# Full 128-row transposes and 64x64 feed-forward tiles in an RWKV-7 and hardswish kernel

## The chip, the cores and the metric

The kernel runs on one core of one Trainium2 chip. The metric is the device time of one execution in microseconds, taken as the median of several runs; less is better. One profiled execution stands beside the runs, and all rows below come from it.

## The reference

There are two parts. The first is a recurrence over 768 time steps, for 4 batches of 8 heads of width 40. The second is a feed-forward layer over its 3072 output rows. All of it is float32.

```python
for t in range(S):                       # state: (B, H, D, D), D = 40
    y[:, :, t] = einsum('bhd,bhde->bhe', rt, state)
    Sa = einsum('bhde,bhe->bhd', state, at)
    state = state * wt[:, :, None, :] - einsum('bhd,bhe->bhde', Sa, bt) \
          + einsum('bhd,bhe->bhde', vt, kt)
# x = y as (B*S, H*D) = (3072, 320)
h = x @ w_in                             # 320 x 2048
out = (h * clip(h + 3, 0, 6) / 6) @ w_out   # 2048 x 320
```

## The kernel before

**Units.** The 768 steps are cut into 12 blocks of 64. A unit is one block of 64 steps for two batches (128 rows: two batches of 64 steps) and all 8 heads; there are 24 units, in six groups of four (NU = 4). Inside a unit the recurrence is solved as matrix products: decay products along the block (stages W, gam), turned copies of the inputs (stages A, B, K, RT, VT, S, factor), scores between them (F, E, C, H), the inverse of a triangular matrix for the whole group (invert, on VectorE, and third_block, on TensorE), the solved vectors (U, UT), the output (rS, y) and the new state (in y).

**Turning.** TensorE turns an input from rows of time to rows of features with a transpose against an identity. turn_pairs (L524) does it with four 128x128 transposes into one bank. turn_halves (L534) does it with eight 64-row transposes, one per batch, into a pair of banks. turn_in chooses by a flag. The same choice stands, written out, in factor_stage (L703 halves, L708 full) and in s_S (L943 halves, L946 full). Units 4 and later take halves in RT and VT, units 8 and later in B, factor and S (A in units 8 to 11), units 12 and later in K. From unit 8 the inputs R, and from unit 12 the inputs A, are turned by VectorE instead (L475, L478).

**Feed-forward.** feed_forward is a generator of TensorE pieces. A unit has two jobs. A job expands (L1147, tile h): for each of two column halves c, eight 128x128 products on the features 0 to 255 (two row groups), and then the last 64 features (function short): eight products of 64 rows, from win2, with c = 0 on partitions 0 to 63 and c = 1 on 64 to 127. Then ScalarE (L1162) and VectorE (L1163) make gt, and contract (L1188, tile o) multiplies by w_out, eight products of 320 columns. Tile h has room for one job, so the next job's L1147 waits for this job's L1163. The list narrow holds the waiting short of a job; it may be called ahead of its turn.

**The steady part.** From unit 4 each unit is four blocks; block m runs parts of the unit being solved (own) and of a unit being prepared (ahead). Blocks are written out by together: it goes through a list of stage names (TURNS first, then one of two NARROW lists), calls each stage up to its TensorE work, and keeps count of PSUM banks. Five are there for it: a bank one, and two pairs of two banks. A stage in TURNS takes the bank one, then halves of a pair; a stage in NARROW takes part of a pair. When five would be exceeded, finish is called: all stages begun so far issue their copies out of PSUM, in the order of the list RESULTS, and the count starts again. At the end of a block finish is called as well. Between the blocks, feed issues as many feed-forward pieces as the digit of GAPS says, and after each piece as many VectorE steps of the inversion (L803, L809) as the digit of INVERSION says. Every engine executes its own instructions in the order in which they were issued.

**Queues.** Stage move issues four copies of the finished output into the feed-forward's input xt from ScalarE's queue (L1091), and move2 four more from SP's; stage beside issues one from SP's (L1031); fetch issues the input loads, on SP's queue in the steady part.

The choice of where short goes, in together, and the count of banks for a turn:

```python
            if name == NARROW[order][0] and narrow and spread[0] and stages:
                narrow[0]()
            for stage in stages.get(name, []):
                if name in TURNS:
                    need = 2 * (open_half[0] is None) if ring[0][0] == "pair" else 1
```

Of the kernel before, what the change touches and what calls it, by code (L numbers as in the profile page):

```python
# [16 lines left out]
P = 128  # L17
# [3 lines left out]
SLOT = 64  # L21
# [10 lines left out]
def kernel(  # L32
# [42 lines left out]
    nc = tc.nc  # L75
    B, H, T, D = r.shape
# [501 lines left out]

    def prepare(i, F):
        n, o = i % NU, data[i]  # L580
        halves = i >= 2 * NU
        def w_stage():
            wt = turn_pairs(o["WN"])
            yield PE
# [145 lines left out]
                fetch(name, following(i))  # L730

        def k_stage():
            by_halves = i >= 3 * NU
            x = turn_in(o["KN"], by_halves)
            yield PE
            kt = o["kt"] = turned("kt")
            for y, z, g in zip(parts_of(kt, by_halves), x, parts_of(o["rg"], by_halves)):
                nc.vector.tensor_tensor(out=y, in0=z, in1=g, op=ALU.mult)
# [143 lines left out]
    def step(i):  # L882
# [8 lines left out]
        def s_RT():  # L891
            m["RT"] = turned("RT")
            if blocked("R", i):
                turn_blocks(m["RT"], o["RN"], "R")
            else:
                x = turn_in(o["RN"], halves)
                yield PE
                for y, z in zip(parts_of(m["RT"], halves), x):
                    nc.scalar.activation(out=y, in_=z, func=AF.Copy)
            if i:  # L900
                fetch("R", i + 1)
            if fresh:
                nc.gpsimd.tensor_copy(last_dec[p][:], dec[:, 1])
                return
            scale = tmp.tile([P, 2, NPR], F32, name="scale", bufs=2)
            nc.gpsimd.tensor_tensor(out=scale[:], in0=last_dec[p][:], in1=dec[:, 0], op=ALU.mult)
            nc.gpsimd.tensor_copy(last_dec[p][:], dec[:, 1])
            nc.vector.tensor_tensor(out=st[:, :, :, 0:D], in0=st[:, :, :, 0:D],
                                    in1=_ap(scale[:], 0, [[NPR, 2], [1, NPR], [0, D]]), op=ALU.mult)
# [15 lines left out]
            nc.vector.tensor_tensor(out=R, in0=rp[2], in1=o["EV"][:], op=ALU.add)  # L925

        def s_VT():
            x = turn_in(VN, halves)
            yield PE
            m["VT"] = turned("VT")  # L930
            for y, z in zip(parts_of(m["VT"], halves), x):
                nc.scalar.activation(out=y, in_=z, func=AF.Copy)  # L932

        def s_S():

            halves = i >= 2 * NU
            sp = ps_pair(4, SLOT) if halves else ps_any([P, 2, 2, P])
            for q in range(2):
                for j in range(2):
                    x = st[:, q, 2 * j:2 * j + 2, :].rearrange("p r d -> p (r d)")  # L940
                    if halves:
                        for s in range(2):
                            nc.tensor.transpose(out=sp[s][:, 2 * q + j, :], in_=x[half(s)],  # L943
                                                identity=ident[half(s), half(s)])
                    else:
                        nc.tensor.transpose(out=sp[:, q, j, :], in_=x, identity=ident[:])  # L946
            yield PE
            S = m["S"] = grp.tile([P, 2, 2, P], F32, name="S", tag="S", bufs=1)
            if halves:
                nc.scalar.activation(out=S[:].rearrange("p q j (s e) -> p s (q j) e", s=2), in_=sp[2], func=AF.Copy)  # L950
            else:
                nc.scalar.activation(out=S[:], in_=sp[:], func=AF.Copy)
# [188 lines left out]
    def expand(xt, j0, gts):  # L1141

        hp = [pools["h"].tile([P, NQ, P], F32, name="h", tag="h", bufs=2) for _ in range(2)]
        begun = [0, 0]

        def add(c, i, lhsT, rhs):
            nc.tensor.matmul(out=hp[c][:, i, :], lhsT=lhsT, rhs=rhs, start=(begun[c] == 0),  # L1147
                             stop=(begun[c] == 3 * NQ - 1))
            begun[c] += 1

        def short():
            narrow.clear()
            for i in range(NQ):
                for c in range(2):
                    add(c, i, win2[half(c), (j0 + i) * P:(j0 + i + 1) * P], xt[half(c), 2, :])
            if begun[0] + begun[1] == 6 * NQ:
                results()

        def results():
            for c in range(2):  # L1160
                gt = ffn.tile([P, NQ, P], F32, name="gt", bufs=4)
                nc.scalar.activation(out=gt[:], in_=hp[c][:], func=AF.Relu, bias=three[:], scale=1.0)  # L1162
                nc.vector.scalar_tensor_tensor(out=gt[:], in0=gt[:], scalar=6.0, in1=hp[c][:],  # L1163
                                               op0=ALU.min, op1=ALU.mult)
                gts.append(gt)

        narrow.append(short)
        for c in range(2):
            for t in range(2):
                for i in range(NQ):  # L1170
                    j = c * HJ + j0 + i
                    add(c, i, win[:, t, j * P:(j + 1) * P], xt[:, t, :])
                if c == 1 and t == 1 and not narrow:
                    results()
                yield True
        if not spread[0] and narrow:
            short()
            yield True
# [219 lines left out]
    for _ in range(18):  # L1398
# [7 lines left out]
    OWN_STAGES = [["RT", "VT"], ["R", "C", "S", "beside"], ["U", "UT", "rS"], ["H"], ["y"], ["move", "move2"]]  # L1406
    AHEAD_STAGES = [["W", "gam"], ["A", "B"], ["F"], ["K", "factor"], ["E"], [], [], ["EV"]]
    CLOSE_STAGES = [["W", "gam"], ["A", "B"], ["F", "K", "factor"], ["E"], [], ["EV"]]
    TURNS = ["W", "S1", "K1"]
    NARROW = [["RT1", "VT", "A1", "B", "factor", "y", "EV", "R", "C", "U", "UT", "rS", "H", "E", "F", "K", "S"],  # L1410
             ["B", "A1", "S", "VT", "E", "U", "K", "C", "y", "factor", "H", "R", "UT", "RT1", "rS", "EV", "F"]]
    RESULTS = ["C", "S", "RT1", "RT", "VT", "y", "S1", "R", "W", "A1", "move", "A", "EV", "B", "move2", "U",
              "UT", "rS", "K", "H", "K1", "factor", "E", "gam", "F", "beside"]
    FIRST_OTHER = {"RT": 2 * NU, "A": 3 * NU, "K": 3 * NU, "S": 2 * NU}
    WIDTH = {"R": NPR * D, "U": NPR * D, "y": NPR * BOTH, "EV": NPR * D}
    BLOCKS = 4
# [1 line left out]
    def together(stages, order):  # L1418
# [14 lines left out]
        for name in products:  # L1433
            if name == NARROW[order][0] and narrow and spread[0] and stages:
                narrow[0]()
            for stage in stages.get(name, []):
                if name in TURNS:
                    need = 2 * (open_half[0] is None) if ring[0][0] == "pair" else 1
                else:
                    width = WIDTH.get(name, NPR * BL)  # L1440
                    need = 2 * (shared[0] is None or shared[1] + width > 512)
                if banks + need > 5:
                    finish()
                    banks, need = 0, 1 if name in TURNS else 2
                banks += need
                rest = stage()
                next(rest)
                begun.append((name, rest))
# [36 lines left out]
    for t in (by_v, by_u):  # L1485
        nc.gpsimd.memset(t[:, :, 0:BL], 0.0)
    del score[1:]
    GAPS = "71052314311277562421243135343899422124213525759654324442543253966531154234264363"
    INVERSION = "00000000000034230000000000221223000000000012232300000000001323230000000000122343"
    m = 0  # L1490
    for i in range(NU, NK):
        spread[0] = i >= 2 * NU - 1
# [54 lines left out]
```

## Time and profile before

| what | value |
|---|---|
| runs, median (lowest to highest) | 791.65 us (790.71 to 793.52) |
| span of the profiled execution | 791.4 us |
| TensorE busy | 719.5 us, 91% of the span |
| VectorE busy | 507.2 us, 64% |
| ScalarE busy | 298.1 us, 38% |
| feed-forward, 128-row expand (L1147) | 1536 instructions, mean 282 ns |
| feed-forward, 64-row expand (L1147) | 768 instructions, mean 294 ns |
| feed-forward, contract (L1188) | 768 instructions, mean 443 ns |
| halved turns L534, L703, L943 | 448, 128 and 128 transposes |

The page gives no time of the profiled execution apart from its span; the span lies 0.2 us under the median of the runs. A float32 product shows as two TensorE instructions, a transpose as one. The mean time of a TensorE instruction is longer than the step from one to the next, since they overlap: what a group costs is read from the start of the group to the start of the next. The share of busy time is not the same all along: over the stretch from 332.7 to 791.4 us TensorE is busy for 451.8 of 458.7 us, over the one from 195.5 to 332.7 us for 125.0 of 137.2 us.

### The profile page before, as it was taken

How to read it: one execution, taken by the hardware profiler on the slowest of the kernel's cores; microseconds unless marked ns; L12 is line 12 of the kernel's file. 1: busy time of each engine (PE TensorE's matmuls, PEld its weight loads, DVE VectorE, ACT ScalarE, POOL GpSimd, SP SyncE). 2: the span in 40 equal slices, each digit the busy share in tenths (PEclk: the TensorE clock that was granted, in tenths of full speed). 3: DMA queues.
4: the chain of work that ended last, by engine and by line, in shares of the span. 5: the costliest groups of instructions: out<-in, count | busy, mean ns of one | idle time of the engine just before them, and what ended most of it. 6: DMA issues, size and time to landing. Idle time of an engine off the chain costs nothing.

```text
span 791.4 us, 32710 instructions
## 1 busy us (share of the span) xinstructions
PE 719.5 (91%) x14440; PEld 608.4 (77%) x14440; DVE 507.2 (64%) x1018; ACT 298.1 (38%) x632; POOL 166.5 (21%) x312
## 2 busy tenths in 40 slices
PE   4725778999899898999999999999999999999998
PEld 3625676878778786888888888888888888888886
DVE  7898877689455598655698556997436892233110
ACT  2347653221544422542423553234453323422111
POOL 6403012421222321222202222213212201000000
PEclk9856879999999899999999999999999999999999
DMA  9683653420334421444331344323332201211000
GB/s 122 126 193 86 155 141 59 79 45 9 53 70 72 77 53 32 84 78 85 65 64 34 76 79 94 66 47 64 67 69 58 47 14 42 46 38 28 20 9 17
DMA packets 196414, 52.74 MB, mean 67 GB/s; under 512 B 179632, under 2 KB 194992, under 8 KB 196272
## 3 DMA queue, kind: packets, MB, share of 16 engines
q1 hardware_dynamic: 188648, 47.28, 31.0%
q10 hardware_dynamic: 7624, 3.36, 1.6%
q8 instruction: 114, 1.87, 1.0%
q14 instruction: 28, 0.23, 0.1%
HBM read 38.67 MB, written 3.93 MB: 54 GB/s over the span
## 4 chain that ended last, share of the span: by engine, by line
PE 71%; DVE 15%; issue 4%; DMA 3%; ACT 2%; SPq 2%; POOL 0%; ACTq 0%; DVEq 0%; POOLq 0%
PE h L1147 25%; PE o L1188 24%; PE pair L562 4%; PE pair L1043 3%; DVE prod L803 3%; DVE x L809 3%; PE pair L534 2%; SPq L508 2%; DMA raw<-in_moe_w_out_dram 2%; PE pair L961 2%; PE one L524 1%; DVE prods L599 1%; PE pair L997 1%; PE pair L981 1%; PE pair L921 1%
## 5 line engine op out<-in xcount | busy, mean ns | idle before, releaser
L1147 PE MATMUL h<-xt,win 128*128 128x128 f32 (+1 forms) x2304 | 252.1, 286 | 5.8 <-DVE gt L1163 5.8
L1147 PEld LDWEIGHTS h<-xt,win 128*128 128x128 f32 (+1 forms) x2304 | 233.7, 195 | 22.7 <-DVE gt L1163 7.0
L1188 PE MATMUL o<-wout,gt 128*128 128x320 f32 x768 | 229.7, 443 | 0.8 <-ACT ys L1003 0.8
L1188 PEld LDWEIGHTS o<-wout,gt 128*128 128x128 f32 x768 | 139.3, 191 | 52.3 <-issue 1.1
L1163 DVE SCALAR_TENSOR_TENSOR gt<-gt,h 128x512 f32<-128x512 f32 x96 | 61.6, 682 | 107.2 <-ACT gt L1162 107.2
L1162 ACT ACTIVATE gt<-h,three 128x512 f32<-128x512 f32 x96 | 61.4, 684 | 135.1 <-PE h L1147 115.1
L803 DVE TENSOR_TENSOR prod<-x 128x30 f32<-128x30 f32 (+9 forms) x180 | 66.8, 371 | 6.5 <-POOL x L788 1.3
L809 DVE TENSOR_TENSOR x<-x,prod 128x30 f32<-128x30 f32 (+9 forms) x180 | 65.0, 361 | 5.9
L575 DVE COPY_PREDICATED store<-mask,pair 128x512 f32<-128x512 int32 x40 | 29.2, 730 | 54.8 <-PE pair L562 41.5
L1051 POOL TENSOR_TENSOR yg<-ys,gam 128x512 f32<-128x512 f32 x20 | 25.4, 1272 | 149.7 <-DVE ys L1050 87.2
L723 POOL TENSOR_TENSOR KBt<-K,rgt 128x320 f32<-128x320 f32 x19 | 16.7, 880 | 149.9 <-ACT rgt L712 146.3
L599 DVE TENSOR_TENSOR_SCAN prods<-wm,start 128x528 f32<-128x528 f32 x24 | 34.1, 1428 | 12.4 <-ACT wm L596 12.0
L1043 PE MATMUL pair<-store,KBt 64*64 64x104 f32 x1280 | 32.6, 251 | 0.6 <-ACT F L693 0.6
L610 DVE TENSOR_TENSOR_SCAN wm<-wm,start 128x528 f32<-128x528 f32 x24 | 30.6, 1277 | 0.8
L1043 PEld LDWEIGHTS pair<-store,KBt 64*64 64x64 f32 x1280 | 29.2, 133 | 1.5 <-ACT F L693 0.7
L757 ACT ACTIVATE EV<-pair 64x320 f32<-64x320 f32 x44 | 18.9, 430 | 28.8 <-PE pair L752 25.2
L642 POOL TENSOR_TENSOR at<-at,gam 128x512 f32<-128x512 f32 x12 | 15.2, 1269 | 65.5 <-DVE at L478 61.5
L950 ACT ACTIVATE S<-pair 128x512 f32<-128x512 f32 x16 | 9.6, 597 | 48.1 <-DVE store L575 27.2
L932 ACT ACTIVATE VT<-pair 128x512 f32<-128x512 f32 x22 | 13.1, 598 | 33.4 <-PE pair L562 18.0
L871 ACT ACTIVATE tinv<-pair 32x256 f32<-32x256 f32 x48 | 17.9, 374 | 19.3 <-PE pair L861 15.3
L1206 ACT ACTIVATE ob<-o 128x320 f32<-128x320 f32 x22 | 9.6, 437 | 40.7 <-issue 25.9
L783 DVE STREAM_TRANSPOSE fb<-F 128x1024 f32<-128x1024 f32 x6 | 13.0, 2159 | 17.8 <-ACT F L693 15.7
(289 smaller groups left out, 1044.7 us busy)
## 6 DMA issues: line engine op xcount, KB each, us to landing
R<-in_r_dram SPq DMA_DIRECT2D x156, 40.0 KB
A<-in_a_dram SPq DMA_DIRECT2D x61, 80.0 KB
V<-in_v_dram SPq DMA_DIRECT2D x96, 40.0 KB
out_dram<-ob SPq DMA_DIRECT2D x47, 80.0 KB
B<-in_b_dram SPq DMA_DIRECT2D x42, 80.0 KB
store<-V SPq DMA_DIRECT2D x20, 160.0 KB
W<-in_w_dram SPq DMA_DIRECT2D x37, 80.0 KB
K<-in_k_dram SPq DMA_DIRECT2D x37, 80.0 KB
```

Source lines behind the costliest of these rows:

```text
L562: nc.tensor.matmul(out=o[i][half(q), n, :], lhsT=lhs[half(i, D), n ^ (2 * q * swap), half(q)], rhs=rhs[half(i, D), n ^ (2 * q * back), hal ...
L575: nc.vector.copy_predicated(out=x[:, :, 0:BL].rearrange("p (h i) t -> p i h t", i=2), mask=mask8, data=o[2])
L599: nc.vector.tensor_tensor_scan(out=prods[:].rearrange("p r m i -> p (r m i)"), data0=wm[:, 0:SCAN], data1=start[:], initial=0.0, op0=ALU.m ...
L610: nc.vector.tensor_tensor_scan(out=back, data0=back, data1=start[:], initial=0.0, op0=ALU.mult, op1=ALU.add)
L803: nc.vector.tensor_tensor(out=pv, in0=_ap(x[:], (i + 1) * L + i, [[L, n], [0, i]]), in1=_ap(x[:], i * L, [[0, n], [1, i]]), op=ALU.mult,)
L809: nc.vector.tensor_tensor(out=rest, in0=rest, in1=pv, op=ALU.add)
L1043: nc.tensor.matmul(out=y[q][half(s), pr, :], lhsT=o[name][half(q), h * D:h * D + SLOT], rhs=m[name][half(q), x, :], start=(name == "K" and ...
L1051: nc.gpsimd.tensor_tensor(out=yg[:], in0=m["ys"][:].rearrange("p r q t -> p r (q t)"), in1=o["G"][:], op=ALU.mult)
L1147: nc.tensor.matmul(out=hp[c][:, i, :], lhsT=lhsT, rhs=rhs, start=(begun[c] == 0), stop=(begun[c] == 3 * NQ - 1))
L1162: nc.scalar.activation(out=gt[:], in_=hp[c][:], func=AF.Relu, bias=three[:], scale=1.0)
L1163: nc.vector.scalar_tensor_tensor(out=gt[:], in0=gt[:], scalar=6.0, in1=hp[c][:], op0=ALU.min, op1=ALU.mult)
L1188: nc.tensor.matmul(out=op[:], lhsT=gts[c][:, n, :], rhs=wout[:, c * HJ + r * NQ + n, :], start=((split or r == 0) and c == 0 and n == 0), ...
```

## The change

- The flags of the halved turns are set to False, so all turns from unit 4 on that TensorE makes are four 128x128 transposes (L524, L708, L946).
- short issues sixteen products of 64 rows by 64 columns instead of eight of 64 rows by 128 columns: each of the former is cut in two column halves z. The 128 moving columns stay.
- TURNS now holds ten names, so in a block the turns come first, then short, then the products; both NARROW lists and RESULTS have a new order.
- A turn that would take the bank one while the count is not zero forces finish (1 + 5 * (banks > 0)).
- GAPS and INVERSION have other digits.

```diff
     def prepare(i, F):
         n, o = i % NU, data[i]
-        halves = i >= 2 * NU
+        halves = False
...
         def k_stage():
-            by_halves = i >= 3 * NU
+            by_halves = False
...
-                x = turn_in(o["RN"], halves)
+                x = turn_in(o["RN"], False)
...
         def s_VT():
-            x = turn_in(VN, halves)
+            x = turn_in(VN, False)
...
         def s_S():
-            halves = i >= 2 * NU
+            halves = False
...
         def short():
             narrow.clear()
             for i in range(NQ):
+                for z in range(2):
+                    for c in range(2):
+                        j = (j0 + i) * P
+                        nc.tensor.matmul(out=hp[c][half(z), i, :], lhsT=win2[half(c), j + z * SLOT:j + (z + 1) * SLOT],
+                                         rhs=xt[half(c), 2, :], start=(begun[c] == 0),
+                                         stop=(begun[c] == 3 * NQ - 1))
                 for c in range(2):
-                    add(c, i, win2[half(c), (j0 + i) * P:(j0 + i + 1) * P], xt[half(c), 2, :])
+                    begun[c] += 1
...
-    TURNS = ["W", "S1", "K1"]
-    NARROW = [["RT1", "VT", "A1", "B", "factor", "y", "EV", "R", "C", "U", "UT", "rS", "H", "E", "F", "K", "S"],
-             ["B", "A1", "S", "VT", "E", "U", "K", "C", "y", "factor", "H", "R", "UT", "RT1", "rS", "EV", "F"]]
-    RESULTS = ["C", "S", "RT1", "RT", "VT", "y", "S1", "R", "W", "A1", "move", "A", "EV", "B", "move2", "U",
-              "UT", "rS", "K", "H", "K1", "factor", "E", "gam", "F", "beside"]
+    TURNS = ['RT1', 'A1', 'W', 'B', 'S', 'K1', 'VT', 'factor', 'S1', 'K']
+    NARROW = [['UT', 'E', 'C', 'U', 'H', 'EV', 'R', 'F', 'y', 'rS'], ['y', 'C', 'U', 'E', 'UT', 'H', 'EV', 'R', 'rS', 'F']]
+    RESULTS = ['C', 'RT', 'beside', 'S1', 'R', 'E', 'A1', 'RT1', 'factor', 'A', 'K1', 'B', 'move', 'UT', 'EV', 'W', 'U', 'move2', 'rS', 'K', 'S', 'y', 'gam', 'H', 'VT', 'F']
...
-                    need = 2 * (open_half[0] is None) if ring[0][0] == "pair" else 1
+                    need = 2 * (open_half[0] is None) if ring[0][0] == "pair" else 1 + 5 * (banks > 0)
...
-    GAPS = "71052314311277562421243135343899422124213525759654324442543253966531154234264363"
-    INVERSION = "00000000000034230000000000221223000000000012232300000000001323230000000000122343"
+    GAPS = '80052314141177681321243134362899422124213425759654314542433363975621173033562253'
+    INVERSION = '00000000000033230000000000221223000000000012232310010000002312330000010000131334'
```

More of the change, by code (lines that the diff above doesn't have):

```diff
@@ L895, in s_RT @@
             else:
-                x = turn_in(o["RN"], halves)
+                x = turn_in(o["RN"], False)
                 yield PE
-                for y, z in zip(parts_of(m["RT"], halves), x):
+                for y, z in zip(parts_of(m["RT"], False), x):
                     nc.scalar.activation(out=y, in_=z, func=AF.Copy)
@@ L927, in s_VT @@
         def s_VT():
-            x = turn_in(VN, halves)
+            x = turn_in(VN, False)
             yield PE
             m["VT"] = turned("VT")
-            for y, z in zip(parts_of(m["VT"], halves), x):
+            for y, z in zip(parts_of(m["VT"], False), x):
                 nc.scalar.activation(out=y, in_=z, func=AF.Copy)
         def s_S():
-            halves = i >= 2 * NU
+            halves = False
             sp = ps_pair(4, SLOT) if halves else ps_any([P, 2, 2, P])
```

## The prediction

> **What bounds the kernel.** I read the busy shares first, then the busy time of each engine by stretch, then TensorE's timeline.
>
> ```profile
> PE 719.5 (91%) x14440; PEld 608.4 (77%) x14440; DVE 507.2 (64%) x1018; ACT 298.1 (38%) x632; POOL 166.5 (21%) x312
> ...
> PE 71%; DVE 15%; issue 4%; DMA 3%; ACT 2%; SPq 2%; POOL 0%; ACTq 0%; DVEq 0%; POOLq 0%
> ```
>
> The second line is the chain that ended last. By stretch (busy time of PE, PEld, DVE, ACT, POOL, then the granted clock):
>
> ```profile
> 195.50:217.60 22.10, 19.10 (x503) 16.05 (x501) 11.09 (x19) 12.81 (x28) 7.12 (x12) 1.00 0.27 47
> 217.60:247.00 29.40, 28.01 (x654) 22.40 (x652) 15.69 (x30) 12.53 (x31) 8.11 (x14) 1.00 0.43 77
> 247.00:272.50 25.50, 23.19 (x546) 19.48 (x544) 12.65 (x23) 12.38 (x31) 7.27 (x14) 0.87 0.38 69
> 272.50:332.70 60.20, 54.68 (x1077) 46.21 (x1077) 50.28 (x107) 20.64 (x44) 14.51 (x26) 0.97 0.30 57
> 332.70:791.40 458.70, 451.80 (x8632) 381.24 (x8628) 255.11 (x508) 160.61 (x349) 79.92 (x139) 1.00 0.27 53
> ```
>
> From 332.7 us on TensorE is the bound: a microsecond more of its work is one more of time. I call this stage E. The four before it, A to D, hold units 4 to 8; TensorE waits in them, and twice its clock is granted at half. Before 195.5 us only the form of short differs, beside VectorE's chain (the L803 and L809 steps fill VectorE until 193.5 us); I cost that at nothing, and at 14 x 0.1 = 1.4 us of gain if TensorE were the bound there.
>
> Timeline, TensorE alone:
>
> ```profile
> 508.39 1.16 PE L1147 MATMUL h<-xt,win 64*128 64x128 f32 x16
> 509.39 0.41 PE L534 MATMUL pair<-ident,B 64*128 64x64 f32 x8
> 509.63 0.41 PE L943 MATMUL pair<-ident,state 64*128 64x64 f32 x8
> 509.98 0.69 PE L562 MATMUL pair<-RT,VT 40*64 40x64 f32 x32
> ...
> 218.77 0.60 PE L524 MATMUL one<-ident,W 128*128 128x128 f32 x4
> 219.21 3.40 PE L1188 MATMUL o<-wout,gt 128*128 128x320 f32 x12
> ...
> 499.85 1.61 PE L1043 MATMUL pair<-store,KBt 64*64 64x104 f32 x64
> 501.39 1.34 PE L1188 MATMUL o<-wout,gt 128*128 128x320 f32 x4
> ```
>
> From start to start: short takes 1.00 us, a halved turn 0.24 (followed by the same shape) or 0.35 (followed by 64x64 tiles), so a change of shape costs about 0.10. A full turn followed by full-size work takes 0.44. y takes 1.54.
>
> **The parts of the change.**
>
> Turns: 448 + 128 + 128 halved transposes, 8 to a turn, are 88 turns. Each costs 0.44 instead of 0.24: +0.20, together +17.6 us of TensorE; 62 of them lie in E, +12.4. The copies out of PSUM keep their sizes.
>
> Changes of shape: a halved turn stood between full-size work and 64x64 products, a third shape. In the built programs the changes between neighbours fall from 343 to 275, of these 47 in E: -4.7 us. [...]
>
> Short: 32 instructions instead of 16. No row has 64x64 tiles of 128 columns. The nearest is y: 64 instructions of 104 columns in 1.44 us without the change after it, 22.5 ns each. Scaled by 128/104 that is 27.7 ns, 0.89 us a short, -0.11. From below, 22.5 ns as it stands: 0.72, -0.28. From above, as if the halves did not run abreast, today's 62.5 ns each: 2.00, +1.00. With 34 shorts in E: -3.7 us, bounds -9.5 and +34. I take -3.7, since y uses the same four tiles in the same rotation.
>
> So E has 12.4 - 4.7 - 3.7 = +4.0 us of work. Its waits before (groups whose start-to-start time is over the sum of their instructions) add up to 4.8 us, the largest 1.1 at 394 us and 0.9 at 341.8. In the new order the turns for C are copied earlier, which ends the first kind (1.6 us). New ones come from RESULTS: S is now copied after move. Units with a third_block in their second block make L861 reuse the pair of S. I put E's waits at 2.5, that is -2.3. E: +1.7.
>
> Stage A, first block of unit 4. R is now turned ahead of W, both into the bank one, and the new count forces finish between them. In the built program W's transpose waits for ScalarE's copy of R. That copy stands behind other work:
>
> ```profile
> 195.71 2.12 ACT L824 ACTIVATE tinv<-tb 32x1024 f32<-32x1024 f32 x2 [7.99 <-DVE tb L812]
> 197.87 1.26 ACT L1162 ACTIVATE gt<-h,three 128x512 f32<-128x512 f32 x2
> 199.02 0.60 ACT L899 ACTIVATE RT<-pair 128x512 f32<-128x512 f32 x1
> ```
>
> R's turn ends at 196.1, its copy at 199.62: TensorE idles 3.5 us, with V and eight feed-forward products behind W. W's copy and scan start only 0.3 us later than before, so the chain on VectorE is hardly late, and the moved work fills waits that were there (1.4 at 206.9, 0.5 at 212, 1.4 at 213; of which 0.85 and 0.7 remain). Following each instruction to the next short I get 2.1 us late at 218.6 instead of 216.5, the five turns of A included. The other end for this wait is nothing, were the copy of R issued ahead. Then the clock:
>
> ```profile
> 302.50:306.00 3.50, 0.47 (x4) 0.47 (x5) 3.31 (x9) 0.00 (x0) 0.00 (x0) 1.00 0.24 37
> 306.00:309.40 3.40, 3.40 (x31) 3.18 (x29) 2.90 (x11) 0.00 (x0) 0.00 (x0) 0.50 0.00 0
> ...
> 305.53 3.71 PE L1147 MATMUL h<-xt,win 128*128 128x128 f32 x24 [3.78 <-DVE gt L1163]
> ```
>
> After an idle stretch of 3.78 us the clock is 0.50 for 3.4 us, which costs 1.7. I expect the same after 3.5 us idle. A: +3.8.
>
> Stage B (units 4 and 5): nine turns +1.8, four changes and two shorts fewer -0.6; waits of 2.0 become 1.3: +0.5.
>
> Stage C: now L997 waits 1.71 us at 260.36 for VectorE's L571, which stands behind L599, which waits for wm on ScalarE behind move's issues; then the clock is 0.50 from 261.6 to 268.4, 3.4 us lost. RESULTS now puts L571 ahead of L599, and a short stands in between. New waits: L752 for the copies of y (+0.65, as the feed-forward piece after y is gone), K and factor for L648 and L656 behind gt (+1.0). With its turns, C takes 22.8 us instead of 25.5: -2.7.
>
> Stage D: the 3.78 us above and its half clock go almost wholly, since gt now stands after the step with 11x20 elements in the inversion, six steps of about 0.4 us earlier. What is late next is unit 8: W's copies stand behind L824, and L599 now ahead of y's L1050, so E waits 0.7 us and L838 1.8 (0.65 before) for y's pair; then L861 waits 1.6 for S behind four issues of move (L1091, 3.53 us for four at 324.92). Summed to the end of L683: -2.1.
>
> Queues: on ScalarE move is issued ahead of S, so xt is not later; what waits behind it is the copy of S, and for that L861. On SP, beside (L1031) now stands ahead of the fetches of its block; it waits for VN and the earlier y, which are done, and its issue took 0.67 us at 296.74; the inputs are used a block later. GAPS and INVERSION move pieces between blocks; their number is the same. POOL gets nothing new; its L1051 follows L1050, up to 1.3 us later behind L599, which move's wait takes in.
>
> Sum: A +3.8, B +0.5, C -2.7, D -2.1, E +1.7 = +1.2 us, against the trace's span of 791.4, which lies 0.2 under the median 791.65. Forecast 792.9 us, own range 789 to 797. What the measurement can tell from no change is about 0.3%, 2.4 us.
>
> **Rivals.**
>
> 1. Slower: the copy of S behind move. If all eight units with a third_block pay 1.6 us at L861 as I have it for unit 8, six more than I counted pay about 1.5: +9, 802. It decides when the four issues and S (4.1 us) outlast the work from L838 to L861. For it: the 3.53 us row. Against it: in units 12 to 21 the built order has 5.3 to 6 us of TensorE work there. Chance 0.22.
>
> 2. Faster: TensorE arrives later at every copy, since each full turn adds 0.2 us, so the new waits of C and D (1.65 and 4.1 us) never arise: 792.9 - 5.7 = 787.2. For it: waits of E before were few with a like supply. Against it: the named copies stand behind fixed work on the same engine. Chance 0.17.
>
> 3. The column halves do not run abreast: +34 and +3.7, 831. Against it: y's 22.5 ns. Chance 0.02.
>
> 4. Full transposes lower the clock. A turn of W and V is 0.9 us; if each of the 20 units lost one half-clock window of 1.7 us, +34: 827. Against it: full turns of W stand in E at a clock of 1.00. [...] Chance 0.02.
>
> That the change does nothing is out, as the built programs differ from unit 4 on.
>
> **How the numbers follow.** The forecast has 0.57. Within it, 0.05 falls below 789.3, 0.31 within 789.3 to 794.0, 0.21 above. Rival 1 is slower; rival 2 faster but for 0.03; 3 and 4 slower. Faster: 0.05 + 0.14 = 0.19; slower: 0.21 + 0.22 + 0.04 = 0.47; same: 0.34. The range takes in rivals 1 and 2 up to 802 and down to 787; about 0.1 lies above, under 0.1 below.
>
> **What would show it.** Right: an L524 turn at 0.44 us start to start; short at 0.89; about 3.5 us idle ahead of W near 196 us, then a half clock; no wait of over 1 us on L571 near 260 or on gt near 305; waits at L838 and L861 in unit 8. Wrong: short near 0.7 or 2.0; L861 waiting in every unit with a third_block; clocks under 1.00 in E; many waits of L946 on VectorE, since L599 now stands ahead of L908.

## The result, and the profile after

The changed kernel takes 801.9 us (median of four executions, 800.3 to 805.4) where the kernel before, on the same chip, takes 792.6 (790.7 to 796.2): a ratio of 1.0113, interval 1.0074 to 1.0152. A second measurement of the same pair (the run e9_again below) gave 1.0156, interval 1.0130 to 1.0181. So the change costs 9 to 12 us. The profiled execution took 800.3 us, with a span of 798.6 against 791.4.

The page of the changed kernel, the lines that answer to the first two shown of before (busy time of the engines; the chain that ended last):

```profile
PE 721.9 (90%) x14856; PEld 614.9 (77%) x14856; DVE 501.0 (63%) x1018; ACT 298.3 (37%) x632; POOL 167.4 (21%) x312
...
PE 52%; issue 2%; DMA 2%; SPq 2%; DVE 1%; ACT 0%; POOL 0%; ACTq 0%; DVEq 0%; POOLq 0%
```

TensorE is still the bound. It has 416 matmuls more and only 2.4 us more of busy time, so two thirds of the lost 7.2 us are idle time. The stages A to E, cut at the same pieces of work as in the prediction (the short ahead of unit 4's last feed-forward pieces, the y of units 5 and 6, the end of L683 in unit 8); busy time of PE, PEld, DVE, ACT and POOL, then the granted clock:

```profile
195.50:221.80 26.30, 20.73 (x470) 17.75 (x470) 10.16 (x17) 11.21 (x23) 7.10 (x12) 0.87 0.24 42
221.80:253.90 32.10, 30.17 (x672) 24.48 (x664) 17.07 (x32) 14.91 (x38) 7.99 (x14) 1.00 0.38 68
253.90:276.00 22.10, 20.92 (x534) 17.82 (x532) 13.10 (x24) 11.88 (x29) 7.92 (x16) 1.00 0.42 77
276.00:335.60 59.60, 54.53 (x1121) 46.26 (x1121) 50.05 (x106) 20.81 (x44) 14.11 (x23) 1.00 0.31 61
335.60:798.60 463.00, 454.19 (x8922) 387.02 (x8920) 249.68 (x508) 160.26 (x348) 79.88 (x139) 1.00 0.26 52
```

With the ends of before at 216.5, 247.0, 272.4 and 332.7 us, and TensorE's last instruction at 787.2 instead of 794.4:

| stage | before | after | difference | predicted |
|---|---|---|---|---|
| A, unit 4 | 21.0 | 26.3 | +5.3 | +3.8 |
| B, units 4 and 5 | 30.5 | 32.1 | +1.6 | +0.5 |
| C, unit 5 to 6 | 25.4 | 22.1 | -3.3 | -2.7 |
| D, to unit 8 | 60.3 | 59.6 | -0.7 | -2.1 |
| E, the rest | 454.5 | 458.8 | +4.3 | +1.7 |
| sum | | | +7.2 | +1.2 |

Stages A, B and C hold the same feed-forward work before and after. Four contract products (L1188, L1194 after the change), 0.28 us each from one to the next, fall into D after the change and into E before it: at equal work D would have gained about 1.8 us and E lost about 5.4.

Two stages hold the loss. In A, TensorE's timeline shows the wait that was forecast, ahead of W's turn. The kernel before, and under it the changed kernel:

```profile
195.53 0.66 PE L524 MATMUL one<-ident,W 128*128 128x128 f32 x4
196.12 0.47 PE L534 MATMUL pair<-ident,R 64*128 64x64 f32 x8
196.42 0.41 PE L534 MATMUL pair<-ident,V 64*128 64x64 f32 x8
```

```profile
195.47 0.65 PE L524 MATMUL one<-ident,R 128*128 128x128 f32 x4
199.79 0.66 PE L524 MATMUL one<-ident,W 128*128 128x128 f32 x4 [3.67 <-ACT RT L899]
200.28 0.94 PE L524 MATMUL pair<-ident,V 128*128 128x128 f32 x4
```

In E there is something that the trace of before shows only in two small cases, both in stage A: TensorE stops in the middle of a group of equal products, and the profile names no releaser ("issue"). The two of before, of 0.46 and 0.47 us from start to start, and a group of L683 in E that runs through:

```profile
211.47 0.43 PE L981 MATMUL pair<-tinv,RR 64*64 64x64 f32 x12
212.14 0.51 PE L981 MATMUL pair<-tinv,RR 64*64 64x64 f32 x18 [0.24 <-issue]
...
215.35 0.39 PE L562 MATMUL pair<-at,kt 40*64 40x64 f32 x11
216.00 0.57 PE L562 MATMUL pair<-at,kt 40*64 40x64 f32 x21 [0.25 <-issue]
...
518.79 0.65 PE L683 MATMUL pair<-bt,at 40*64 40x64 f32 x32
```

The changed kernel at 525 us, the products behind a short:

```profile
522.87 0.63 PE L961 MATMUL pair<-RR,tinv 64*64 64x40 f32 x32
523.30 0.67 PE L981 MATMUL pair<-tinv,RR 64*64 64x64 f32 x32
523.80 0.65 PE L997 MATMUL pair<-RT,S 40*64 40x64 f32 x32
524.26 0.57 PE L683 MATMUL pair<-bt,at 40*64 40x64 f32 x25
525.56 0.34 PE L683 MATMUL pair<-bt,at 40*64 40x64 f32 x7 [0.73 <-issue]
```

From start to start the gap is 0.94 us, between two instructions of one kind, and the profile shows nothing that the second waits for. There are four such gaps in E, 4.1 us together, and one of 1.2 in D; before has none over 0.3 us in E. They are not spread at random. Count TensorE's instructions in order (weight loads, matmuls and the 320 instructions that only wait on semaphores): each gap lies at place 192 or 193 of a stretch of 256, and so do the two of before. The page of the profile lists the queues with kind, packets, MB and share; the larger of two that it calls instruction:

```profile
q8 instruction: 117, 1.92, 1.0%
```

These are packets of 16 KB; TensorE's 30,035 instructions over 117 of them are 257 each.

The packets around the gaps, from the trace (us):

| load begins | load lands | gap ends | gap | in |
|---|---|---|---|---|
| 332.35 | 333.78 | 335.06 | 1.19 | L683 |
| 442.65 | 443.56 | 445.04 | 0.75 | L861 |
| 447.64 | 448.58 | 449.94 | 1.36 | L683 |
| 463.17 | 464.17 | 465.66 | 1.03 | L921 |
| 523.07 | 524.28 | 525.56 | 0.94 | L683 |

Each gap ends 1.3 to 1.5 us after a block has landed. So the suspicion, not yet shown by these two traces, is that TensorE runs out of instructions: by my estimate a block of 256 holds some 127 pairs of load and matmul, which at 15 ns (32 matmuls of L683 in 0.47 us) are gone in 1.9 us, while 2.3 to 2.7 us pass from the beginning of a load to the end of the gap.

### The profile page after: what moved, and what is told of

It is laid out like the page before. It is cut to its first block, busy times and chain, and to the rows that moved or that the text cites. A ratio compares the mean times of both kernels' runs of the same rounds, so it can differ in the third digit from the quotient of the medians.

```text
span 798.6 us, 33491 instructions
## 1 busy us (share of the span) xinstructions
PE 721.9 (90%) x14856; PEld 614.9 (77%) x14856; DVE 501.0 (63%) x1018; ACT 298.3 (37%) x632; POOL 167.4 (21%) x312
## 4 chain that ended last, share of the span: by engine, by line
PE 52%; issue 2%; DMA 2%; SPq 2%; DVE 1%; ACT 0%; POOL 0%; ACTq 0%; DVEq 0%; POOLq 0%
PE o L1194 18%; PE h L1147 15%; PE h L1157 4%; PE pair L1043 3%; PE pair L562 2%; PE one L524 1%; PE pair L961 1%; PE pair L524 1%; PE pair L981 1%; PE pair L997 1%; PE pair L921 1%; PE pair L683 1%; PE pair L861 1%; PE pair L838 1%; PE pair L752 1%
## 5 line engine op out<-in xcount | busy, mean ns | idle before, releaser
L1194 PE MATMUL o<-wout,gt 128*128 128x320 f32 x768 | 229.1, 443 | 0.0
L1147 PE MATMUL h<-xt,win 128*128 128x128 f32 x1536 | 195.5, 282 | 4.1 <-DVE gt L1169 3.6
L1147 PEld LDWEIGHTS h<-xt,win 128*128 128x128 f32 x1536 | 184.0, 194 | 12.9 <-DVE gt L1169 4.4
L1194 PEld LDWEIGHTS o<-wout,gt 128*128 128x128 f32 x768 | 139.9, 191 | 51.7 <-issue 2.2
L803 DVE TENSOR_TENSOR prod<-x 128x30 f32<-128x30 f32 (+9 forms) x180 | 64.0, 355 | 7.2 <-POOL x L788 1.9
L1157 PE MATMUL h<-xt,win 64*64 64x128 f32 x1536 | 53.8, 277 | 0.2 <-issue 0.2
L1157 PEld LDWEIGHTS h<-xt,win 64*64 64x64 f32 x1536 | 42.0, 134 | 8.2 <-issue 5.5
L599 DVE TENSOR_TENSOR_SCAN prods<-wm,start 128x528 f32<-128x528 f32 x24 | 30.0, 1258 | 12.4 <-ACT wm L596 12.3
L1043 PE MATMUL pair<-store,KBt 64*64 64x104 f32 x1280 | 32.7, 251 | 0.5 <-ACT F L693 0.5
L1043 PEld LDWEIGHTS pair<-store,KBt 64*64 64x64 f32 x1280 | 29.6, 133 | 2.4 <-issue 1.3
L610 DVE TENSOR_TENSOR_SCAN wm<-wm,start 128x528 f32<-128x528 f32 x24 | 30.5, 1273 | 0.8
L738 DVE TENSOR_TENSOR kt<-pair,rgam 128x512 f32<-128x512 f32 x15 | 10.3, 684 | 29.4 <-PE pair L524 29.4
L987 ACT ACTIVATE UT<-pair 128x512 f32<-128x512 f32 x22 | 13.1, 595 | 36.7 <-PE pair L981 35.1
L757 ACT ACTIVATE EV<-pair 64x320 f32<-64x320 f32 x44 | 18.9, 430 | 20.3 <-PE pair L752 14.7
```

What stands on the lines that cost most here:

```text
L599: nc.vector.tensor_tensor_scan(out=prods[:].rearrange("p r m i -> p (r m i)"), data0=wm[:, 0:SCAN], data1=start[:], initial=0.0, op0=ALU.m ...
L610: nc.vector.tensor_tensor_scan(out=back, data0=back, data1=start[:], initial=0.0, op0=ALU.mult, op1=ALU.add)
L803: nc.vector.tensor_tensor(out=pv, in0=_ap(x[:], (i + 1) * L + i, [[L, n], [0, i]]), in1=_ap(x[:], i * L, [[0, n], [1, i]]), op=ALU.mult,)
L1043: nc.tensor.matmul(out=y[q][half(s), pr, :], lhsT=o[name][half(q), h * D:h * D + SLOT], rhs=m[name][half(q), x, :], start=(name == "K" and ...
L1157: nc.tensor.matmul(out=hp[c][half(z), i, :], lhsT=win2[half(c), j + z * SLOT:j + (z + 1) * SLOT], rhs=xt[half(c), 2, :], start=(begun[c] = ...
L1194: nc.tensor.matmul(out=op[:], lhsT=gts[c][:, n, :], rhs=wout[:, c * HJ + r * NQ + n, :], start=((split or r == 0) and c == 0 and n == 0), ...
```

## The experiments

Each kernel has one profile, and the median of several executions against the kernel before on the same chip. "Gaps" are pauses over 0.3 us at borders of blocks, after 340 us; "unit 10 to end" goes from its y (L1043) to TensorE's last instruction.

| run | what | ratio to before, interval | span | y of unit 4 | unit 10 to end | gaps | half clock, windows begun from 125 to 780 us |
|---|---|---|---|---|---|---|---|
| before | | | 791.4 | 223.2 | 398.1 | 0 | 10.2 |
| after | the change | 1.0113, 1.0074 to 1.0152 | 798.6 | 229.1 | 402.3 | 4.1 | 6.8 |
| e9_again | the change | 1.0156, 1.0130 to 1.0181 | 803.1 | 231.1 | 404.0 | 4.7 | 17.0 |
| e1_shift | 116 instructions more | 1.0112, 1.0081 to 1.0144 | 802.6 | 231.9 | 399.4 | 1.3 | 27.2 |
| e2_no_wait | W freed, V caught | 1.0144, 1.0115 to 1.0174 | 801.0 | 228.9 | 403.4 | 5.1 | 13.6 |
| e5_ring | W and V freed | 1.0075, 1.0050 to 1.0100 | 797.5 | 222.4 | 406.8 | 5.8 | 13.6 |
| e8_ring_shift | e1 and e5 | 1.0008, 0.9960 to 1.0056 | 790.9 | 224.3 | 398.6 | 0.9 | 10.2 |
| e10_ring_4 | e5, 16 more | 1.0057, 1.0030 to 1.0085 | 796.6 | 225.3 | 403.6 | 4.0 | 13.6 |
| e3_old_short | short undone | 1.0157, 1.0121 to 1.0193 | 798.6 | 228.4 | 403.4 | 0.4 | 3.4 |
| e4_halves | turns undone | 1.0043, 1.0015 to 1.0072 | 797.9 | 227.6 | 401.6 | 1.7 | 20.4 |
| e6_b_short | short alone | 0.9997, 0.9966 to 1.0027 | 791.5 | 222.2 | 401.2 | 0 | 13.6 |
| e7_b_both | short, E ahead of W | 0.9986, 0.9955 to 1.0017 | 791.8 | 224.4 | 397.9 | 1.7 | 13.6 |
| e11_y_first | e8, y ahead of W | 1.0076, 1.0052 to 1.0100 | 797.0 | 225.2 | 402.3 | 0.4 | 0 |
| e12_b_gaps | e7, new spread | 1.0033, 1.0012 to 1.0055 | 797.1 | 226.2 | 398.6 | 2.5 | 27.2 |

In e1, e8, e10 and e11 the lines from L555 on stand four further down (L566 is L562, L687 is L683).

### Where the blocks begin: e1_shift, e9_again, e10_ring_4

Twenty-nine products of unit 0 are issued twice, into the same place:

```
+    again = [58]
     def scores(lhs, rhs, swap=False, back=False):
...
+                    for _ in range(2 if again[0] > 0 else 1):
+                        again[0] -= 1
                         nc.tensor.matmul(out=o[i][half(q), n, :],
```

The count of 29 was chosen from the trace of the changed kernel, so that few borders fall behind a dense stretch.

> The changed kernel with 29 products of the first unit (L562) issued twice, which adds 58 weight loads and 58 matmuls (116 of TensorE's instructions) long before 130 us and nothing after. Theory: TensorE's instructions arrive in blocks of 256, and the pauses inside groups in the changed kernel (0.29 us at 329.7, 1.2 at 335.1, 0.75 at 445.0, 1.35 at 449.9, 1.0 at 465.7, 0.9 at 525.6) are blocks that landed too late; moved by 116 instructions the blocks begin in slower stretches, nearly all these pauses go, and the span falls from 798.6 to 793-796 us. Rival: the pauses belong to these products (a bank or a copy that comes late): they stay at the same products, and the span stays at 798-800.

The gaps near 335, 445, 450 and 526 us are gone; of the 1.0 us near 466 the next border makes 0.8 and 0.5 (469 and 473 us). From unit 10 to the end the time falls from 402.3 to 399.4, by 2.9 us, where the gaps fall by 2.8. The theory holds for E, and the rival falls, as nothing else was moved there. But the span did not fall: it is 802.6. Ahead of unit 10, 27.2 us ran at half clock instead of 6.8, and its y came 6.9 us later. Why is not shown by this run. The executions reach from 799.1 to 804.3, and the ratio, 1.0112, is that of the changed kernel.

> The changed kernel once more, unaltered. Theory: the pauses at block borders are set by the program and stay at the same instructions (0.7 to 1.9 us each near 335, 445, 450, 466 and 526 us, 4 to 7 us together), and so do the 3.5 us of idle time ahead of W; which stretches run at half clock behind them differs from look to look, as the windows of 3.41 us lie otherwise. Ratio to the kernel before 1.008 to 1.015. Rival: the pauses are chance, and in this look they lie elsewhere or are gone.

The theory held in the main. In another execution of the same program the gaps lie again in L861, L683 and L683 (447.6, 453.0 and 530.0 us: 0.5, 1.9 and 1.8); those near 335 and 466 are missing, and one of 0.5 at 352.2 is new, all at borders of blocks. So in these two executions the gaps stand at borders of blocks alone, and three of them in the same lines; whether one stands there, and how long it is (those three 0.75, 1.36 and 0.94 us in the first execution), differs between the two. The ratio came out at 1.0156, just above what was expected. This execution has 17.0 us of half clock instead of 6.8, which at half speed is up to 5.1 us of loss, and a span 4.5 us longer: the two executions of one program differ in their windows at half clock by about as much as its times do (800.3 to 806.6).

> The banks for turns set anew and four products of the first unit issued twice instead of 29: 16 more of TensorE's instructions, not 116. Theory: what counts is where the blocks of 256 begin, so the pauses of the last stage stay (near 440, 445 and 520 us, 4 to 6 us together), and the span is 795-799 like that of the kernel without doubled products. Rival: doubled products early on help in some other way: few pauses, span 789-793.

As the theory has it: 4.0 us of gaps (346.0, 441.7, 447.4 and 561.8 us, the last in place of that at 520), span 796.6. With sixteen instructions more 4.0 us of gaps stay, with 116 (e8_ring_shift) 0.9. This excludes that doubling products helps in itself.

### The wait for R's copy: e2_no_wait, e5_ring, e8_ring_shift

The first attempt took away the forced finish in the first block:

```
-need = 2 * (open_half[0] is None) if ring[0][0] == "pair" else 1 + 5 * (banks > 0)
+need = 2 * (open_half[0] is None) if ring[0][0] == "pair" else 1 + 5 * (banks > 0 and m > 0)
```

> The changed kernel without the forced finish between the turns of R and W in the first block of unit 4: W goes into a pair of banks and does not wait for ScalarE's copy of R. Theory: the idle 3.7 us ahead of W at 199.8 and the half clock behind it go, and with the work in better order the second half clock at 217.5 too; the y of unit 4, at 229.1 us in the changed kernel and 223.2 in the one before, comes at 223.5-225, and the span is 793-795. Rival: W's scan on VectorE is late anyway, so the idle time only moves to the products of this unit: y at 227-229, span 797-799.

It missed its aim. Timeline of TensorE in e2_no_wait:

```profile
194.99 0.66 PE L524 MATMUL one<-ident,R 128*128 128x128 f32 x4
195.48 0.60 PE L524 MATMUL pair<-ident,W 128*128 128x128 f32 x4
199.31 1.11 PE L524 MATMUL one<-ident,V 128*128 128x128 f32 x4 [3.23 <-ACT RT L899]
```

The list of banks stood at its second place when the stage began, so W got the pair and V the bank one, and V waits for R's copy just as W had. The y of unit 4 gains 0.2 us. That looks like the rival, but the idle time never went away, so neither is tested. The next kernel sets the list anew:

```
+    ring.clear()
+    ring.extend(TURNS_IN)
     m = 0
     for i in range(NU, NK):
```

> The changed kernel with the banks for turns set anew ahead of the first block of unit 4, so that R is turned into the bank one and W and V into the two halves of a pair: none of the three waits for ScalarE's copy of R, and nothing else moves. Theory: the 3.7 us of idle time at 196-200, which went to V when only W was freed, goes altogether, with the half clock behind it (1.7 us): y of unit 4 at 223.5-225.5 instead of 229.1, span 793-796 with the late blocks of the last stage as they are. Rival: the chain over W's scan and the solves sets the end of unit 4, and the idle time moves behind the later products: y at 227.5-229.5, span 797-800.

Timeline of TensorE in e5_ring:

```profile
194.79 0.66 PE L524 MATMUL one<-ident,R 128*128 128x128 f32 x4
195.28 0.60 PE L524 MATMUL pair<-ident,W 128*128 128x128 f32 x4
195.72 0.60 PE L524 MATMUL pair<-ident,V 128*128 128x128 f32 x4
196.16 4.47 PE L1194 MATMUL o<-wout,gt 128*128 128x320 f32 x16
```

The whole wait is gone, and the y of unit 4 starts at 222.4 instead of 229.1, earlier than in the kernel before. Of the 6.7 us, 5.6 are still there at the y of unit 10 (386.5 instead of 392.1). So the chain over W's scan did not set this end, and the rival falls. In E the gaps are longer here, 5.8 us with two windows of half clock right behind them (445.5 and 524.0 us), and they take back most: the span of 797.5 is that of the rival, though not for its reason.

> The changed kernel with the banks for turns set anew ahead of unit 4 and with the 29 products of the first unit issued twice. Theory: both gains add, 4 to 5.5 us up to unit 4's y and 3 to 4 us of late blocks in the last stage (from 402.7 to 399-400 us between the y of unit 10 and the end): span 789-793, about the kernel before. Rival: what is gained ahead of unit 8 is lost again there to further half clocks: span 795-799.

Both gains add: 790.9 us of span, and 398.6 from unit 10 on. The same products as at 525 us in the changed kernel, in e8_ring_shift (L687 is L683):

```profile
516.37 0.62 PE L965 MATMUL pair<-RR,tinv 64*64 64x40 f32 x32
516.81 0.67 PE L985 MATMUL pair<-tinv,RR 64*64 64x64 f32 x32
517.30 0.65 PE L1001 MATMUL pair<-RT,S 40*64 40x64 f32 x32
517.77 0.65 PE L687 MATMUL pair<-bt,at 40*64 40x64 f32 x32
```

With the ring set, the medians are 1.0075 without the shift, 1.0057 with 16 instructions (on another chip) and 1.0008 with 116. The intervals of these overlap, and in e1 the shift alone moved no median. What is shown is the two together: with the wait in A and most of the late blocks gone, the changed kernel is level with the kernel before, to within 0.6%. What each of the two is worth in the median is not shown.

### One part alone, or undone: e3_old_short, e4_halves, e6_b_short

In e3 short has again two matmuls of 64 rows and 128 columns for each i, by `add(c, i, ...)`.

> The changed kernel with short as before: 16 instructions of 64 rows and 128 columns instead of 32 of 64x64; order and turns as changed. Theory: a short costs 1.05-1.15 us instead of 0.925, as it also stands between two other shapes, +4 to +7 us for 34 of them in the last stage; the instruction stream ahead of the products is thinner, so the pauses at block borders (4 us from 330 us on) shrink to under 1.5 us. Span 798-802. Rival: the pauses come from the products' order, not from the stream: they stay at about 4 us, span 802-806.

As the theory has it: a short takes 1.09 us from start to start (0.925 in the changed kernel), the gaps shrink to 0.4 us, and the span is the same 798.6; from unit 10 to the end it takes 403.4 us instead of 402.3. So in these two profiles the dearer short and the missing gaps about cancel. That a thinner stream removes the gaps is not shown: with 768 matmuls fewer the borders of the blocks lie elsewhere too, and e1 shows that this alone removes most of them.

In e4 the flags are as before (`halves = i >= 2 * NU`, `by_halves = i >= 3 * NU`), and the halved turns are counted with the pairs of banks:

```
-                if name in TURNS:
+                if name in TURNS and (u < 2 * NU or name not in HALVED):
```

> The changed kernel with the halved turns as before (from unit 8 on two transposes of 64 rows for each of 128, in pairs of banks counted with the other halved products); 64x64 short and new orders stay. Theory: in the last stage TensorE is the bound, so 62 turns times 0.20 us less, about 45 changes of shape at 0.10 us more: 8 us less, span 789-793; the wait for W at 196 us stays. Rival: the turns are hidden behind waits for copies, or the halved turns bring back those waits: span 796-800.

By the profile the rival was nearer, with a span of 797.9. From unit 10 on the turns take 22.5 us instead of 28.2: 49 of the 56 are halved, 0.12 us less for each, with the change of shape behind it counted in. But the other full-size work takes 262.6 us instead of 257.5. I put that down to one more change of shape at each halved turn and to the 6.8 us of this stretch that ran at half clock; the share of each is not shown. The half clock follows a window, 444.5 to 447.9, in which TensorE was 51% busy, and in that lies a wait of 1.2 us for ScalarE. Timeline of e4_halves:

```profile
444.60 1.34 PE L1194 MATMUL o<-wout,gt 128*128 128x320 f32 x4
445.09 0.60 ACT L950 ACTIVATE S<-pair 128x512 f32<-128x512 f32 x1 [5.47 <-DVE bt L656]
445.58 1.26 ACT L1168 ACTIVATE gt<-h,three 128x512 f32<-128x512 f32 x2
446.72 1.54 ACT L871 ACTIVATE tinv<-pair 32x256 f32<-32x256 f32 x4
447.13 0.30 PE L961 MATMUL pair<-RR,tinv 64*64 64x40 f32 x2 [1.19 <-ACT tinv L871]
```

Its median (796.9) is still 5 us under the changed kernel's. Part of that is not the turns: R and V of unit 4 are halved here too, so W did not wait at 196 us, against what I had expected, and with 352 matmuls more the borders of the blocks lie elsewhere (gaps of 1.7 us instead of 4.1). What the turns alone cost is therefore not settled by this run.

In e6 the new short stands in the kernel before, ahead of its halved turns.

> The kernel before with 64x64 short alone, at its old place ahead of the halved turns. Theory: a short costs 0.92 us instead of 1.00, so 34 x 0.08 = 2.7 us less in the last stage, and 0.5 to 2 us of it are given back where one of TensorE's blocks of 256 instructions comes late, since each short now has 32 more of them: span 788.5-791.5. Rival: the denser stream costs nothing by itself: no pause of over 0.3 us at a block border after 330 us, span 787-788.5.

Both missed the price. A short takes 1.035 us here and not 0.92, as the next instruction is again of another shape; in the changed kernel too the 10 shorts with 128x128 work right behind them take 1.035, and the 35 with 64x64 or 40x64 products 0.925 (medians). From unit 10 on 30 of them take 30.3 us instead of 30.9. There is no gap over 0.3 us, though it has more of TensorE's instructions than the changed kernel (15,208 matmuls). From unit 10 on it takes 3.1 us longer, which is one wait of y for V's transfer and a window of half clock behind it (473.2 us). Timeline of e6_b_short:

```profile
472.47 2.44 PE L1043 MATMUL pair<-store,KBt 64*64 64x104 f32 x64 [1.51 <-DMA store<-V]
```

The ratio is 0.9997. So the 64x64 tiles saved 2.6 us on 30 shorts where 64x64 products followed at once (the changed kernel, 28.3 us) and 0.6 us here, and more instructions alone brought no gap.

### Looking for a kernel that beats both: e7_b_both, e11_y_first, e12_b_gaps

In e7 the kernel before gets the new short, and its RESULTS has "E" ahead of "W".

> The kernel before with 64x64 short, and in the order of the copies the masked copy of E (L571) ahead of W's scan (L599), as the changed kernel has it; halved turns and all else as before. Theory: the wait of 1.9 us at 258 and the half clock from 261.6 to 268.4 go, 2.5 to 3.5 us less up to the y of unit 6 at 272.4, and short saves what it saves alone: span 785.5-789. Rival: the scan is late in its turn and the gain of that stage is lost by unit 8: span 788-791.

The rival's account was right, though the span of 791.8 lies just outside its range. From the y of unit 5 to that of unit 6 it takes 21.2 us instead of 25.4, as the wait for L571 and its half clock are gone. Up to unit 10 the next stage takes 120.3 instead of 116.7, with 10.2 us of half clock from 301.8 on; the y of unit 8 is at 339.3, before at 339.4. Ratio 0.9986, interval 0.9955 to 1.0017: no difference.

In e11, e8 has "y" ahead of "W" in RESULTS.

> The banks set anew, 29 products issued twice, and the addition after y (L1050) ahead of W's scan (L599) in the order of the copies, as it was before the change. Theory: in unit 8 the product L562 and then L838 no longer wait 0.8 and 1.8 us for the pair of y, 2 to 2.6 us less up to the y of unit 10; span 788-790. Rival: W's scan comes 0.7 us later in every unit and the waits move to what needs it: no gain, span 790-793.

The wait at 842 (838 before the shift of lines) fell from 1.7 to 0.5 us, but the turn of the state now waits 0.6 and 1.2 us for VectorE in units 8 and 9. L566 ahead of it (L562 before the shift) still waits 0.6 us, as in e8: the profile puts that down to ScalarE's copy of VT, not to y, against what I had expected. Timeline of e11_y_first:

```profile
320.79 0.74 PE L842 MATMUL pair<-tb,F 32*32 32x32 f32 x64 [0.50 <-DVE state L1059]
...
323.69 0.63 PE L950 MATMUL pair<-ident,state 128*128 128x128 f32 x4 [0.63 <-DVE state L912]
...
345.68 0.66 PE L950 MATMUL pair<-ident,state 128*128 128x128 f32 x4 [1.23 <-DVE score L575]
```

W's scan is 1.3 us of VectorE, and moving it back moves the wait, as the rival said. It was worse than the rival: from unit 6 to 10 it took 117.5 us instead of 116.1, from there on 402.3 instead of 398.6 with only 0.4 us of gaps, and the ratio is 1.0076. So the scan ahead of y, which the prediction charged with up to 2.5 us in unit 8, looks like the better order on the whole; the intervals of the two ratios just touch.

In e12, e7 has GAPS and INVERSION of the changed kernel.

> The kernel before with 64x64 short, the masked copy of E ahead of W's scan, and the changed kernel's spread of feed-forward pieces and steps of the inversion over the blocks; halved turns as before. Theory: the wait for gt near 303 us shrinks from 3.8 us to under 2 and the half clock behind it goes, 2 to 4 us less up to the y of unit 8; span 786-789, ratio 0.993 to 0.997. Rival: with the other spread TensorE runs dry, or waits for copies, in other blocks: span 790-794.

The wait for gt shrank, but only to 2.0 us at 302.0, and 27.2 us ran at half clock. From unit 6 to 10 it took 122.5 us. It went as the rival said, and further: the span of 797.1 lies above its range. No kernel of this study beats the kernel before by more than its interval.

## Why the prediction was right or wrong

The median of 801.9 us fell just inside the upper end of the wide range, which rival 1 had set at 802, and outside the forecast's own 789 to 797. Rival 1's mechanism did not happen, so that agreement is luck. By the profile the sum missed by 6.0 us (+7.2 instead of +1.2). Two steps failed: stage A had one window of half clock too few, and stage E left out the gaps at borders of blocks, 4.1 us.

**Before 195.5 us** nothing moved, as predicted: the first turn of unit 4 starts at 195.47 us instead of 195.53. Only seven shorts lie there, not the fourteen of the bound given, so that bound was 0.7 us and not 1.4.

**Rival 1** did not happen. The copy of S does stand behind move (L952 starts at 328.16, the turn of S ended near 326.8), but L861 of unit 8 starts at 328.89 right behind its feed-forward piece, and in no unit after the fourth does it wait over 0.3 us. The four issues, taken at 3.53 us, needed 3.0 from first to last (325.10 to 328.12), and the copy behind them still ends under the feed-forward piece ahead of L861.

**Stage A** was right in mechanism and short by 1.5 us. The idle time was 3.67 us (3.5 predicted), and the half clock behind it (200.4 to 203.8) was there. A second window of half clock, 217.5 to 220.9, was not in the sum; at half speed it costs 1.7 us, about the whole miss. Two windows of 3.41 us in unit 4 of the changed kernel, and under them two of before:

```profile
214.05:217.46 3.41, 1.85 (x76) 1.57 (x79) 2.72 (x6) 1.60 (x5) 0.00 (x0) 1.00 0.16 27
217.46:220.88 3.42, 3.42 (x132) 3.42 (x136) 0.00 (x0) 1.26 (x3) 1.68 (x2) 0.50 0.03 5
```

```profile
207.00:210.41 3.41, 2.10 (x83) 2.01 (x76) 2.31 (x5) 1.18 (x4) 0.00 (x0) 1.00 0.58 101
210.41:213.82 3.41, 2.52 (x107) 2.01 (x105) 0.69 (x1) 1.34 (x4) 0.00 (x0) 1.00 0.02 5
```

Waits of 1.3 us (L861) and 0.6 us (L981) left TensorE 54% busy in one window, and the next was at half clock. In the kernel before, the same 1.3 us at L861 fell into a window with 62% and the idle time behind it into the next, with 74%, and nothing followed. The prediction counted waits and half clocks as if only a long wait could bring one.

**Stage B** missed 1.1 us: L683 waits 1.1 us at 240.1 for EV's copy (L757), which had been 0.7 us at L861 behind it, and a border of blocks cost 0.4 at 222.6. **Stage C** was right: -3.3 against -2.7, with the clock at 1.00 and L571 no longer late. **Stage D** gained 0.7 instead of 2.1, or about 1.8 at equal work. E waits 0.6 and L838 1.7 us in unit 8, near the 0.7 and 1.8 worked out; the 1.6 us at L861 did not come; the wait for gt, which was to go almost wholly, still idles TensorE for 1.5 us ahead of 305.3; and one gap of 1.2 us lies in this stage.

**Stage E.** The terms of work were right. From unit 10 on, turns take 28.2 us instead of 20.7 (56 of them; +7.5), shorts 28.3 instead of 30.9 (30; -2.6), full-size work 257.5 instead of 261.4 (-3.9). Of the last, 1.9 us are sixteen expand products that fall ahead of unit 10 in the changed kernel; the rest is put down to fewer changes of shape, which no run shows alone. A full turn is 0.44 us (0.53 with smaller tiles behind it), a short 0.925 (0.89 predicted, not 0.72 or 2.00, so rival 3 is out). With the gaps taken out, 402.3 - 4.1 = 398.2 against 398.1, and with the sixteen products counted in the change's work costs about 2 us here, near the +1.7 of the sum. What failed is the term for new waits, 2.5 us: it looked for waits on copies only, and the gaps alone are 4.1 us. The trace of before had shown the sign: the pause at 212 us stands in the prediction as a wait that the moved work would fill, and is one of the two pauses at borders. The instruction stream was never priced, though the change adds 416 matmuls and puts the short right ahead of 128 products of 15 ns; the four gaps take 0.75 to 1.36 us each.

**Rival 4** asked whether full transposes lower the clock in E. In the profile of the changed kernel the clock is 1.00 from 220.9 to 797.7 us, with all turns full, so it falls; in that of e9_again one window in E is at half clock, at 453.5 us, behind a gap of 1.9 us. **Rival 2**, that the new waits of C and D do not arise, falls by the 0.6 and 1.7 us in unit 8, though of its 4.1 us in D the 1.6 at L861 indeed did not arise.

## What to carry to other kernels

Before an edit makes TensorE's instructions smaller and more, count them: the gaps of this case lay where by my estimate 250 of them run in about 2 us. Look there for pauses inside groups that wait for nothing, and see whether they lie 256 instructions apart, as here (place 192 or 193 of 256); then some harmless instructions early in the program, as many as move the borders out of the dense stretches, show what the pauses cost (in e1_shift 116 took away 2.8 us of gaps and 2.9 us of the time from unit 10 on; in e10_ring_4 16 left 4.0 us of gaps). A bank that is turned into while its last copy stands behind other work on ScalarE waits for that work too (3.67 us ahead of W's turn in the changed kernel), and which bank a turn gets can depend on where a rotating list stood (in e2_no_wait V waited 3.23 us in W's stead): set such lists anew where a stage begins. To the length of a wait add what the clock takes behind it: in stage A of the changed kernel waits of 1.3 and 0.6 us that left TensorE 54% busy in a window were followed by one at half clock, 1.7 us lost at half speed; in the kernel before the same 1.3 us, with the idle time behind it in the next window (62% and 74% busy), were followed by none.

## What the runs showed that was not expected

**Blocks of instructions.** In the profiles of this case, 42 pauses of over 0.3 us lie inside a group of small products after 200 us. 39 of them are at place 192 or 193 of 256, where chance would put one pause in 128. In these 39 the load had landed 1.27 to 1.61 us before the pause ended, and had begun 2.2 to 3.0 us before. When a load begins was not explained: some began with the border before, some 2.7 us after it.

**The clock.** In these profiles the granted clock is 1.00 or 0.50 and changes on a grid of 3.41 us, whose place in the span differs from profile to profile (that of the changed kernel lies 0.2 us behind that of the kernel before). Of 2610 such windows at full clock from 130 to 780 us, in all profiles together, the 27 in which TensorE was at most 55.6% busy were all followed by half clock; of the 47 with more, up to 68%, 10 were; of the 2536 above, none. So here 44.4% of idle time in a window was enough each time. A window at half clock was followed by another in some cases although TensorE was busy throughout (261.6 and 265.0 us in the kernel before); what decides that stays open.
